# When the first six local units ask for their values: an attention, expert and mixer kernel on one core

## The chip, the core and the metric

The kernel runs on one core of a Trainium2 chip, as one program. What counts is its device time in microseconds, the median of several executions. The core has a matrix engine (PE, with its weight loads as PEld), VectorE (DVE), ScalarE (ACT), GpSimd (POOL), a queue that issues most transfers (SP), and 16 DMA engines that carry them from memory (HBM) to the on-chip buffer. Every engine works through its own list of instructions in order; semaphores tie the lists together.

## The reference

Three stages follow each other, for 4 sequences of 768 tokens:

```python
for c in range(nc):                                   # 24 chunks of 32 queries, 8 heads of 64
    k_full = concat([mem_k, k[l_start:r_end]])        # 8 memory slots, 16 tokens left, 8 right
    a = softmax(scale * q_c @ k_full.T)
    out[c] = a @ v_full
x = out.reshape(B, S, 512)
for e in range(4):                                    # experts: causal attention, top 2 of 4 per token
    a = softmax(causal(scale * (x @ wq[e]) @ (x @ wk[e]).T))
    y += gate[e] * (a @ (x @ wv[e]) @ wo[e])
u = y + mix(y, U, V)                                  # over the sequence, rank 32
return u + relu(u @ w_ch1) @ w_ch2
```

## The kernel before

The first stage is cut into *units*: one unit is one sequence, two heads and half of the sequence, so 8 per sequence and 32 in all. A unit has a query tile `q_t` (192 KB in the packed form of the first eight), a key tile `k_t` (220 KB) and a value tile `v_t` (288 KB). Its work is: two score groups (`local_scores`, tile `s` on PE, then `a` on VectorE and ACT, sums `rs` on VectorE, a scaling of `a` on GpSimd), two transposes (`local_turn`, tile `tp` on PE, copied to `at`), the values (`local_values`, tile `t` on PE from `at` and `v_t`), and a split of the result into two parts `xh` (ACT) and `xl` (VectorE) (`local_split`). These feed the projections of the second stage, `pqk` and `pv`.

The first six units, all of the first sequence, run in a loop of six rounds ahead of the main loop (`PRO = 6`). Round r calls `rnd` with unit r for loading and scores (`s_unit`), and unit r-1 for transposes and values (`o_unit`, `locs`). From round 2 on the unit's `xh` and `xl` go into the projection at once (`qk_begin`). Between the rounds the weights come in: four pieces of `wqk` of 256 KB (`load_weights` from table `WLOAD`), split into two parts by `split_weights`; two pieces `wvg`, cast on ACT and subtracted on GpSimd; the mixer's U and V (`fetch_mixer`, and `load_mixer`: a decode on ACT and VectorE, tiles `u_s` and `d_t`, then ACT's cast `vs` and twelve copies `v_st`, four on ACT and eight on GpSimd); and `tri_s`, from which VectorE makes `row_s`.

All of these go out on SP's list, except the first keys and the mask, which ACT issues. An issue takes one of eight semaphores in turn and waits until the transfer that had it before has landed, so eight transfers at most are under way. Value tiles of units 0 to 2 lie in a pool of three buffers; those of units 3 to 5 lie in buffers that the main loop uses later (`FIRST_V`). The lists of all engines are not written by hand: a scheduler puts the recorded operations in order when the program is built, so where an operation is recorded can move its neighbours.

Of the kernel before, what the change touches and what calls it, by code (L numbers as in the profile page):

```python
# [8 lines left out]
F32 = mybir.dt.float32  # L9
# [8 lines left out]
B, H, S, D = 4, 8, 768, 64  # L18
# [3 lines left out]
NG = S // GQ  # L22
GK = NMEM + LEFT + GQ + RIGHT
# [12 lines left out]
PRO = 6  # L36
NPACK = 8
NKEEP = 1
NIDLE = 4
WLOAD = {1: ((0,), ()), 2: ((1,), ()), 3: ((2, 3), ()), 5: ((), (0, 1))}  # L40
WSPLIT = {2: ((0,), ()), 3: ((1, 2), ()), 4: ((3,), ()), 5: ((), (0, 1))}
FILL = ((0, 0, 0, 2, 1, 2, 1, 1, 2, 3, 0, 2),
# [8 lines left out]
NVB = 3  # L51
# [64 lines left out]
def tile_chunk_attention__moe_attention__mixer(  # L116
# [20 lines left out]
    nc = tc.nc  # L137
# [287 lines left out]
    TL, TE, TQ = dict(tag="lt", bufs=2), dict(tag="ts", bufs=2), dict(tag="ts", bufs=2)  # L425
    with ExitStack() as p1:
        const = p1.enter_context(tc.tile_pool(name="const", bufs=1))
        loc = p1.enter_context(ExitStack())
        lin = loc.enter_context(tc.tile_pool(name="lin", bufs=NLIN, side="right"))
# [9 lines left out]
        ps = Banks(p1, "psq", "psc")  # L439
# [16 lines left out]
        def load_weights(qk, vg):  # L456
            for kt in qk:
                raws["qk", kt] = cw.tile([128, 512], F32, name="raw", tag="ac", bufs=NAC)
                nc.sync.dma_start(raws["qk", kt], wqk[kt])
            for i in vg:  # L460
                raws["vg", i] = cw.tile([128, 2, 260], F32, name="raw", tag="ac", bufs=NAC)
                nc.sync.dma_start(raws["vg", i], wvg[2 * i:2 * i + 2].rearrange("k p n -> p k n"))
# [37 lines left out]
        xh, xl, half = {}, {}, {}  # L500
        nhalf = [0]
# [4 lines left out]
        FIRST_V = {n: (cw, dict(tag="ac", bufs=NAC)) for n in (3, 4, 5)}  # L506

        def local_load(u):
            b, hp, hf = u
            gs = slice(hf * NG // 2, (hf + 1) * NG // 2)  # L510
            n = nhalf[0]
            qpool, qkw = FIRST_Q.get(n, (lin, dict(bufs=NKB)))
            kpool, kkw = FIRST_K.get(n, (lin, {}))
            vpool, vkw = FIRST_V.get(n, (lin, dict(bufs=NVB)))
            packed = n < NPACK
            q_t = qpool.tile([128, NG // 2, GQ] if packed else [128, NG // 2, 2, GQ], F32, name="q_t", **qkw)
            nhalf[0] += 1
            hold['q', n] = nc.sync.dma_start(q_t, qP[hp, hf] if packed else qT[b, hp][:, gs]).ins
            k_t = kpool.tile([128, KHALF], F32, name="k_t", **kkw)
            (nc.sync if n else nc.scalar).dma_start(k_t, kw[b, hp, hf])  # L520
            if nhalf[0] == 1:
                nc.scalar.dma_start(band_s[:, :2], band)
                for n, (lo, hi) in enumerate(((0, LEFT), (GK - NMEM - RIGHT, GK - NMEM))):
                    (nc.gpsimd.tensor_copy if n else nc.scalar.copy)(band_s[:, 2 + n], band_s[:, n])
                    nc.gpsimd.memset(band_s[:, 2 + n, lo:hi], NEG_LOCAL)
                nc.sync.dma_start(ident_s, ident)
            v_t = vpool.tile([GK, NG // 2, 2, D], F32, name="v_t", **vkw)
            nc.sync.dma_start(v_t, vw[b, hp][:, gs])
            half[u] = dict(packed=packed, q=q_t, k=k_t, v=v_t, a={}, at={}, ins=[])

        def keys(k_t, g):
            at = g // 2 * KPAIR + g % 2 * (GK - NB)
            return k_t[:, at:at + GK]

        def local_scores(u, qd):
            b, hp, hf = u
            w = half[u]
            s = ps.tile([128, 3, GK], F32, name="s", **TL)
            a = lwk.tile([128, 3, GK], F32, name="a")
            nm = sm.tile([128, 3], F32, name="nm")  # L540
            ss = sm.tile([128, 3], F32, name="ss")
            for j in range(3):
                k_g = keys(w["k"], qd * 3 + j)
                for own in (slice(0, 64), slice(64, 128)) if w["packed"] else (slice(0, 128),):
                    last = nc.tensor.matmul(s[own, j, :], w["q"][own, qd * 3 + j], k_g[own], start=True, stop=True).ins  # L545
            for j in range(3):
                g = hf * NG // 2 + qd * 3 + j
                bd = band_s[:, 2 if g == 0 else 3 if g == NG - 1 else g % 2]
                nc.vector.tensor_tensor_reduce(a[:, j, :], s[:, j, :], bd, op0=ALU.add, op1=ALU.min,  # L549
                                               scale=-scale, scalar=-NEG_LOCAL, accum_out=nm[:, j:j + 1])  # L550
            for j in range(3):
                nc.scalar.activation(a[:, j, :], a[:, j, :], AF.Exp, bias=nm[:, j:j + 1], scale=-1.0,  # L552
                                     accum_out=ss[:, j:j + 1])
            rs = sm.tile([128, 3], F32, name="rs")
            nc.vector.tensor_scalar(rs, ss, 1e-9, None, op0=ALU.add)
            nc.vector.reciprocal(rs, rs)  # L556
            nc.gpsimd.tensor_mul(a, a, rs[:, :, None].to_broadcast([128, 3, GK]))  # L557
            w["a"][qd] = a
            if nhalf[0] <= NKEEP and qd:
                keep_warm(last)  # L560

        def keep_warm(after):
            p = ps.tile([128, 512], F32, name="pwarm", **TQ)
            with tc.issue_after(after):
                for _ in range(NIDLE):
                    nc.tensor.matmul(p, warm[:, :128], warm, start=True, stop=True)

        def local_turn(u, qd):
            w = half[u]
            a = w["a"].pop(qd)  # L570
            tp = ps.tile([GK, 3, 128], F32, name="tp", **(TQ if nhalf[0] < PRO else TL))
            for j in range(3):
                nc.tensor.transpose(tp[:, j, :], a[:, j, :], ident_s)  # L573
            at = lwk.tile([GK, 3, 128], F32, name="at", bufs=NLT)
            w["ins"].append((nc.scalar.copy if qd < NLA else nc.vector.tensor_copy)(at, tp).ins)
            w["at"][qd] = at
# [305 lines left out]

        def rnd(new=None, old=None, s_unit=None, o_unit=None, fill1=(), fill2=(), down=None, then=None, late=(), locs=(), at=None):

            def urgent(kind):
                return tc.high_priority(URGENT[kind, *at]) if at and (kind, *at) in URGENT else ExitStack()

            if s_unit:  # L890
                local_load(s_unit)
                if then:
                    load_weights(*then)
                with urgent(0):
                    local_scores(s_unit, 0)
            turned = []
# [34 lines left out]
            def place(items):  # L931
                w = len(items) * 128
                for n, bank in enumerate(banks):
                    if used[n] + w <= 512:
                        used[n] += w
                        return n, bank[:, used[n] - w:used[n]]

            late = sorted(late, key=lambda v: (shared[v][0], shared[v][1]))
            while late:
                items = [v for v in late if v[:2] == late[0][:2] and shared[v][0] == shared[late[0]][0]]  # L940
                at = place(items)
                if at is None:
                    items = items[:1]
                    at = place(items)
                late = [v for v in late if v not in items]
# [73 lines left out]
        units = batch_half(0, 0) + batch_half(0, 1)  # L1019
# [4 lines left out]
        for r in range(PRO):  # L1024
            more = [lambda: qk_begin(0, 0, r - 2, pp)] if 2 <= r < KT + 2 else []
            if r == PRO - 1:
                more += [lambda t=t: v_proj(0, t) for t in range(3)]
            split = [lambda: split_weights(*WSPLIT[r])] if r in WSPLIT else []
            rnd(s_unit=units[r], o_unit=units[r - 1] if r else None, fill1=split, fill2=more, then=WLOAD.get(r), locs=units[r - 1:r] if r else ())
            if r == 3:  # L1030
                fetch_mixer()
            if r == 4:
                nc.vector.memset(rank_s, 0.0)
                nc.sync.dma_start(identb_s, identb)
                nc.sync.dma_start(tri_s, tri)
                nc.vector.memset(row_s[:, :S - 128], 0.0)
                nc.vector.tensor_copy(row_s[:, S - 128:], tri_s)
        load_mixer()
        old, turned, locs = None, [], []
        for b in range(B):  # L1040
# [7 lines left out]
            for r, (pr, i) in enumerate(ROUNDS[b]):  # L1048
                n = FILL[b][r]
                ending[0] = last and r >= 10  # L1050
                f1, f2, work = work[:n][:1], work[:n][1:], work[n:]
                ups, down = [], None
                for c, g, (turn, low, up) in sorted((c, g, MIX[c][g]) for c in range(max(0, b - 1), b + 1) for g in range(2)):
                    at = 12 * (b - c) + r
# [4 lines left out]
                    if at == low:  # L1059
                        assert down is None  # L1060
                        down = c, g
                f1 = ups + f1
                o_unit = s_at.get(r - 1) if r else before
# [4 lines left out]
                if r in SESSIONS[b]:  # L1068
                    rnd((b, pr, i), old, s_at.get(r), o_unit, f1, f2, down, late=now, locs=locs, at=(b, r))
                    turned, locs = wait, []  # L1070
# [3 lines left out]
                old = (b, pr, i)  # L1074
# [33 lines left out]
    with ExitStack() as p2:  # L1108
        hp = None
        wp2 = p2.enter_context(tc.tile_pool(name="wp2", bufs=1))  # L1110
        ps = Banks(p2, "psp", "psf")
# [42 lines left out]
        late = list(range(NEC, NCH))  # L1154
# [3 lines left out]
        for c in late:  # L1158
            nxt = c + 1 if c + 1 < NCH else None
            po = [ps.tile([128, CT], F32, name=f"po{m}", tag=f"po{m}", bufs=1) for m in range(KT)]  # L1160
            for f in range(FA):
# [6 lines left out]
                if nxt is None and f == FS:  # L1168
# [3 lines left out]
                    hp = p2.enter_context(tc.tile_pool(name="hp", bufs=1, side="right"))  # L1172
# [186 lines left out]
```

## Time and profile before

| what | value |
|---|---|
| median of 3 runs | 803.16 us (802.81 to 803.75) |
| the profiled execution | 804.32 us, of which 802.2 us from the first to the last instruction |
| busy: PE, DVE, ACT, POOL | 782.0, 619.5, 498.2, 160.9 us |
| chain of work that ended last | PE 81%, DVE 10%, DMA 4%, ACT 4% |
| granted clock of TensorE, mean | 0.995 |
| transfers on the main queue | 36416 packets, 76.21 MB |

Busy time is the time in which an engine works on at least one instruction. The chain is followed back from the last instruction: at each step to what released it, or to the instruction ahead of it on its engine. A difference between two executions shows first as a shift of like rows in the timelines.

### The profile page before, as it was taken

Reading aid. Unit: us, or ns where it says so; the run is one execution under the profiler, and the core shown is the slowest. Engines: PE = TensorE matmul, PEld = TensorE weight load, DVE = VectorE, ACT = ScalarE, POOL = GpSimd, SP = SyncE. Lnnn points to the kernel's source line nnn. Section 1 sums busy time; section 2 is a strip of 40 time slices with the busy share of each in tenths; the row PEclk is TensorE's granted clock in tenths of the full one; section 3 lists DMA queues with packets and bytes.
Section 4 is the critical chain, followed back from the end, with each engine's and each line's share of the span. In section 5 each row is a group of like instructions: output and inputs, shape, how many; then the busy total and the mean of one; then the engine's idle time right before and its main releaser. Section 6 shows DMA issues by size and latency. Waiting matters only on the chain.

```text
span 802.2 us, 17606 instructions
## 1 busy us (share of the span) xinstructions
PE 782.0 (97%) x6258; PEld 706.9 (88%) x6258; DVE 619.5 (77%) x2029; ACT 498.2 (62%) x1439; POOL 160.9 (20%) x244
## 2 busy tenths in 40 slices
PE   8999999999999998999999999999999999999997
PEld 5789998989989987888788888999999999999996
DVE  6697768887878679895569899989596695875956
ACT  6787767877777656755346668565464564555642
POOL 5554434544434433311000000000000000000000
PEclk9999999999999998999999999999999999999999
DMA  9443242433232132235056543103002030030211
GB/s 292 125 153 110 90 145 78 138 114 113 78 100 75 36 132 100 79 105 178 27 165 215 186 151 112 54 1 132 1 33 100 1 132 1 1 132 1 84 49 53
DMA packets 36791, 77.65 MB, mean 97 GB/s; under 512 B 4192, under 2 KB 12896, under 8 KB 35936
## 3 DMA queue, kind: packets, MB, share of 16 engines
q1 hardware_dynamic: 36416, 76.21, 29.4%
q8 instruction: 49, 0.80, 0.4%
q10 hardware_dynamic: 288, 0.32, 0.1%
q14 instruction: 38, 0.31, 0.1%
HBM read 60.79 MB, written 15.73 MB: 95 GB/s over the span
## 4 chain that ended last, share of the span: by engine, by line
PE 81%; DVE 10%; DMA 4%; ACT 4%; issue 1%; DVEq 0%; POOL 0%; ACTq 0%; SPq 0%
PE acc L1232 25%; PE ph L377 15%; PE t L881 7%; PE po L394 6%; PE pqk L604 6%; PE pv L644 5%; PE tpc L765 4%; PE s L545 3%; DMA raw<-in_w 2%; PE sc L684 2%; PE tp L573 2%; PE sc L686 2%; PE w1p L335 1%; DVE a L549 1%; ACT a L552 1%
## 5 line engine op out<-in xcount | busy, mean ns | idle before, releaser
L1232 PE MATMUL acc<-xhi,sw 128*128 128x256 f32 x1008 | 187.9, 282 | 0.1
L1232 PEld LDWEIGHTS acc<-xhi,sw 128*128 128x128 f32 x1008 | 159.3, 189 | 4.8 <-ACT xhi L1150 0.3
L1232 PE MATMUL acc<-xlo,sw 128*128 128x256 f32 x504 | 139.1, 282 | 0.2 <-DVE xlo L1151 0.2
L1147 DVE TENSOR_TENSOR sx<-t 128x256 f32<-128x256 f32 x180 | 67.5, 419 | 67.7 <-ACT t L1140 67.6
L1140 ACT ACTIVATE t<-ph 128x512 f32<-128x512 f32 x72 | 43.1, 598 | 100.3 <-PE ph L377 100.3
L1232 PEld LDWEIGHTS acc<-xlo,sw 128*128 128x128 f32 x504 | 95.5, 189 | 2.4 <-DVE xlo L1151 0.4
L1150 ACT CAST xhi<-sx 128x256 fp32r<-128x256 f32 x205 | 74.8, 407 | 22.1 <-DVE sx L1147 19.6
L742 POOL TENSOR_SCALAR ac<-ac,su,g 128x128 f32<-128x128 f32 (+5 forms) x92 | 68.1, 750 | 98.1 <-DVE su L740 33.6
L552 ACT ACTIVATE a<-a,nm 128x96 f32<-128x96 f32 x192 | 69.8, 366 | 16.9 <-DVE nm L549 16.4
L1151 DVE TENSOR_TENSOR xlo<-sx,xhi 128x256 fp32r<-128x256 f32 x205 | 76.5, 418 | 3.0 <-ACT xhi L1150 2.2
L377 PE MATMUL ph<-zh,wp_l 128*128 128x512 f32 x192 | 61.2, 398 | 0.0
L377 PE MATMUL ph<-zh,wp_h 128*128 128x512 f32 x192 | 60.9, 394 | 0.0
L707 ACT ACTIVATE ac<-ac,nmc 128x128 f32<-128x128 f32 (+5 forms) x72 | 47.9, 666 | 15.7 <-DVE nmc L705 15.2
L557 POOL TENSOR_TENSOR a<-a,rs 128x288 f32<-128x288 f32 x64 | 43.2, 679 | 68.2 <-DVE rs L556 21.0
L377 PE MATMUL ph<-zl,wp_h 128*128 128x512 f32 x176 | 55.5, 394 | 0.0
L765 PE MATMUL tpc<-ident_s,ac 128*128 128x128 f32 x336 | 52.3, 276 | 2.8 <-POOL kl L632 1.4
L545 PE MATMUL s<-k_t,q_t 128*128 128x96 f32 (+1 forms) x480 | 51.2, 267 | 2.7 <-DMA k_t<-in_kw 1.8
L545 PEld LDWEIGHTS s<-k_t,q_t 128*128 128x128 f32 (+1 forms) x480 | 46.2, 171 | 6.7 <-PE tp L573 2.2
L684 PE MATMUL sc<-kl,qs 128*128 128x384 f32 (+2 forms) x144 | 48.0, 338 | 2.1 <-DVE ath L767 1.0
L705 DVE CUSTOM_DVE_ANT_0 ac<-sc,row_s 128x128 f32<-128x128 f32 (+5 forms) x72 | 43.2, 617 | 5.0 <-PE sc L686 4.3
L765 PEld LDWEIGHTS tpc<-ident_s,ac 128*128 128x128 f32 x336 | 39.1, 142 | 8.9 <-issue 2.8
L549 DVE CUSTOM_DVE_ANT_0 a<-s,band_s 128x96 f32<-128x96 f32 x192 | 39.6, 250 | 7.1 <-PE s L545 6.3
(210 smaller groups left out, 1949.5 us busy)
## 6 DMA issues: line engine op xcount, KB each, us to landing
raw<-in_w SPq DMA_DIRECT2D x42, 256.0 KB, 3.7
v_t<-in_vw SPq DMA_DIRECT2D x32, 288.0 KB, 3.7
q_t<-in_qT SPq DMA_DIRECT2D x24, 384.0 KB, 3.2
k_t<-in_kw SPq DMA_DIRECT2D x31, 220.0 KB, 3.5
part<-o SPq DMA_DIRECT2D x24, 256.0 KB, 2.6
pt<-part SPq DMA_DIRECT2D x6, 1024.0 KB, 4.8
out<-pt SPq DMA_DIRECT2D x24, 256.0 KB, 2.3
raw<-in_w SPq DMA_DIRECT2D x11, 512.0 KB, 4.6
```

The costliest lines, as they stand in the source:

```text
L377: nc.tensor.matmul(p, w[f // 4][:, pr, fs], z[:, pr], start=(n == 0), stop=(n == 5))
L394: nc.tensor.matmul(po, w[f][:, ms], x, start=(start and n == 0), stop=(stop and n == 2))
L545: last = nc.tensor.matmul(s[own, j, :], w["q"][own, qd * 3 + j], k_g[own], start=True, stop=True).ins
L552: nc.scalar.activation(a[:, j, :], a[:, j, :], AF.Exp, bias=nm[:, j:j + 1], scale=-1.0, accum_out=ss[:, j:j + 1])
L684: nc.tensor.matmul(s[:, o:o + w], q, kl[b, e, hf][:, :w], start=True, stop=False)
L742: (nc.vector if ending[0] else nc.gpsimd).tensor_scalar(aa[h][:, :n], aa[h][:, :n], su[:, h:h + 1], gates[b, i // 3][:, i % 3, 2 * pr + h: ...
L765: hold['t', ROUNDS[b].index((pr, i))] = nc.tensor.transpose(tp[h][:, j * 128:(j + 1) * 128], aa[h][:, j * 128:(j + 1) * 128], ident_s).ins
L881: session.append(nc.tensor.matmul(*a, **kw).ins)
L1147: nc.vector.tensor_tensor(x, t[:, p[0], p[1]], t[:, q[0], q[1]], op=op)
L1150: nc.scalar.copy(hi, x)
L1151: nc.vector.tensor_sub(lo, x, f32(hi))
L1232: ended[0] = nc.tensor.matmul(acc[n][:, m], w[:, ms], x, start=(f == FA and u == 0 and m == 0), stop=(f == NF - 2 and u == 2 and m == 1)).ins
```

## The change

The table `WLOAD` becomes `LOADS`: for each of the six rounds a list of what is loaded, in that order, ahead of `rnd`: keys with queries (`'k'`), values (`'v'`) and weights (`'w'`), the first two with the number of the unit. `local_load` is split into `local_keys` and `local_v`, and keeps its name as a function that `rnd` still calls; it loads what the unit doesn't have yet. The unit's number is kept in its record, and two conditions that looked at the running count now look at that. Nothing else changes in the program's text.

```diff
--- before.py
+++ after.py
@@ -37,7 +37,7 @@
 NPACK = 8
 NKEEP = 1
 NIDLE = 4
-WLOAD = {1: ((0,), ()), 2: ((1,), ()), 3: ((2, 3), ()), 5: ((), (0, 1))}
+LOADS = {0: (('k', 0),), 1: (('k', 1), ('v', 0), ('w', ((0,), ()))), 2: (('k', 2), ('v', 1), ('w', ((1,), ()))), 3: (('k', 3), ('v', 2), ('w', ((2, 3), ()))), 4: (('k', 4), ('v', 3), ('v', 4)), 5: (('k', 5), ('v', 5), ('w', ((), (0, 1))))}
 WSPLIT = {2: ((0,), ()), 3: ((1, 2), ()), 4: ((3,), ()), 5: ((), (0, 1))}
 FILL = ((0, 0, 0, 2, 1, 2, 1, 1, 2, 3, 0, 2),
         (1, 2, 1, 1, 2, 0, 1, 1, 2, 0, 2, 1),
@@ -506,12 +506,17 @@
         FIRST_V = {n: (cw, dict(tag="ac", bufs=NAC)) for n in (3, 4, 5)}
 
         def local_load(u):
+            if u not in half:
+                local_keys(u)
+            if 'v' not in half[u]:
+                local_v(u)
+
+        def local_keys(u):
             b, hp, hf = u
             gs = slice(hf * NG // 2, (hf + 1) * NG // 2)
             n = nhalf[0]
             qpool, qkw = FIRST_Q.get(n, (lin, dict(bufs=NKB)))
             kpool, kkw = FIRST_K.get(n, (lin, {}))
-            vpool, vkw = FIRST_V.get(n, (lin, dict(bufs=NVB)))
             packed = n < NPACK
             q_t = qpool.tile([128, NG // 2, GQ] if packed else [128, NG // 2, 2, GQ], F32, name="q_t", **qkw)
             nhalf[0] += 1
@@ -524,9 +529,13 @@
                     (nc.gpsimd.tensor_copy if n else nc.scalar.copy)(band_s[:, 2 + n], band_s[:, n])
                     nc.gpsimd.memset(band_s[:, 2 + n, lo:hi], NEG_LOCAL)
                 nc.sync.dma_start(ident_s, ident)
-            v_t = vpool.tile([GK, NG // 2, 2, D], F32, name="v_t", **vkw)
-            nc.sync.dma_start(v_t, vw[b, hp][:, gs])
-            half[u] = dict(packed=packed, q=q_t, k=k_t, v=v_t, a={}, at={}, ins=[])
+            half[u] = dict(packed=packed, n=nhalf[0] - 1, q=q_t, k=k_t, a={}, at={}, ins=[])
+
+        def local_v(u):
+            b, hp, hf = u
+            vpool, vkw = FIRST_V.get(half[u]["n"], (lin, dict(bufs=NVB)))
+            v_t = half[u]["v"] = vpool.tile([GK, NG // 2, 2, D], F32, name="v_t", **vkw)
+            nc.sync.dma_start(v_t, vw[b, hp][:, hf * NG // 2:(hf + 1) * NG // 2])
 
         def keys(k_t, g):
             at = g // 2 * KPAIR + g % 2 * (GK - NB)
@@ -556,7 +565,7 @@
             nc.vector.reciprocal(rs, rs)
             nc.gpsimd.tensor_mul(a, a, rs[:, :, None].to_broadcast([128, 3, GK]))
             w["a"][qd] = a
-            if nhalf[0] <= NKEEP and qd:
+            if w["n"] < NKEEP and qd:
                 keep_warm(last)
 
         def keep_warm(after):
@@ -568,7 +577,7 @@
         def local_turn(u, qd):
             w = half[u]
             a = w["a"].pop(qd)
-            tp = ps.tile([GK, 3, 128], F32, name="tp", **(TQ if nhalf[0] < PRO else TL))
+            tp = ps.tile([GK, 3, 128], F32, name="tp", **(TQ if w["n"] < PRO - 2 else TL))
             for j in range(3):
                 nc.tensor.transpose(tp[:, j, :], a[:, j, :], ident_s)
             at = lwk.tile([GK, 3, 128], F32, name="at", bufs=NLT)
@@ -882,15 +891,13 @@
 
 
 
-        def rnd(new=None, old=None, s_unit=None, o_unit=None, fill1=(), fill2=(), down=None, then=None, late=(), locs=(), at=None):
+        def rnd(new=None, old=None, s_unit=None, o_unit=None, fill1=(), fill2=(), down=None, late=(), locs=(), at=None):
 
             def urgent(kind):
                 return tc.high_priority(URGENT[kind, *at]) if at and (kind, *at) in URGENT else ExitStack()
 
             if s_unit:
                 local_load(s_unit)
-                if then:
-                    load_weights(*then)
                 with urgent(0):
                     local_scores(s_unit, 0)
             turned = []
@@ -1026,7 +1033,12 @@
             if r == PRO - 1:
                 more += [lambda t=t: v_proj(0, t) for t in range(3)]
             split = [lambda: split_weights(*WSPLIT[r])] if r in WSPLIT else []
-            rnd(s_unit=units[r], o_unit=units[r - 1] if r else None, fill1=split, fill2=more, then=WLOAD.get(r), locs=units[r - 1:r] if r else ())
+            for kind, n in LOADS.get(r, ()):
+                if kind == 'w':
+                    load_weights(*n)
+                else:
+                    (local_keys if kind == 'k' else local_v)(units[n])
+            rnd(s_unit=units[r], o_unit=units[r - 1] if r else None, fill1=split, fill2=more, locs=units[r - 1:r] if r else ())
             if r == 3:
                 fetch_mixer()
             if r == 4:
```

The built programs differ in their lists only in the prologue; behind it every engine's list is the same. First SP, the issues ahead of the two `wvg` pieces, before (`raw64` are the mixer's U and V; `q_t_465` is unit 4, `q_t_559` unit 5):

```order
L479 DMA raw64_461<-in_mU 128x384
L479 DMA raw64_463<-in_mV 128x384
L518 DMA q_t_465<-in_qP 128x384
L520 DMA k_t_467<-in_kw 128x440
L528 DMA v_t_469<-in_vw 96x768
L1034 DMA identb_s_111<-in_identb 128x128
L1035 DMA tri_s_112<-in_tri 128x128
L518 DMA q_t_559<-in_qP 128x384
L520 DMA k_t_561<-in_kw 128x440
L528 DMA v_t_563<-in_vw 96x768
L462 DMA raw_565<-in_wvg 128x2x260
L462 DMA raw_567<-in_wvg 128x2x260
```

The same stretch after the change, up to the same two pieces:

```order
L523 DMA q_t_471<-in_qP 128x384
L525 DMA k_t_473<-in_kw 128x440
L538 DMA v_t_475<-in_vw 96x768
L538 DMA v_t_477<-in_vw 96x768
L538 DMA v_t_374<-in_vw 96x768
L1046 DMA identb_s_111<-in_identb 128x128
L1047 DMA tri_s_112<-in_tri 128x128
L523 DMA q_t_567<-in_qP 128x384
L525 DMA k_t_569<-in_kw 128x440
L538 DMA v_t_571<-in_vw 96x768
L462 DMA raw_573<-in_wvg 128x2x260
L462 DMA raw_575<-in_wvg 128x2x260
```

There are three value tiles in a row where there was one: `v_t_475` is unit 3's second copy, `v_t_477` unit 4's only one, `v_t_374` unit 2's second one. Nearer the start, after the change, from unit 0's second copy `v_t_202` on:

```order
L538 DMA v_t_202<-in_vw 96x768
L459 DMA raw_204<-in_wqk 128x512
L538 DMA v_t_206<-in_vw 96x768
L523 DMA q_t_277<-in_qP 128x384
L525 DMA k_t_279<-in_kw 128x440
L538 DMA v_t_281<-in_vw 96x768
L459 DMA raw_283<-in_wqk 128x512
L523 DMA q_t_370<-in_qP 128x384
L525 DMA k_t_372<-in_kw 128x440
L538 DMA v_t_285<-in_vw 96x768
L459 DMA raw_376<-in_wqk 128x512
L459 DMA raw_378<-in_wqk 128x512
```

`v_t_202` and `v_t_281` are second copies of units 0 and 1, `v_t_206` and `v_t_285` first copies of units 1 and 2; before, each of these units had one row. The number of a tile grows in the order in which the tiles are made.

Next ACT's list, from the split of unit 1 (`xh_362` before, `xh_366` after) to the copy ahead of unit 3's second transpose (`at_495` before, `at_503` after). Before:

```order
L592 CAST xh_362<-t_349 128x384
L486 CAST vs_765<-d_t_760 128x192
L575 COPY at_400<-tp_396 96x384
L496 CAST v_st_115<-vs_765 32x192 x3
L552 ACTIVATE a_472,ss_474<-a_472,nm_473 128x96 x3
L496 CAST v_st_115<-vs_765 32x192
L471 CAST wvg_h_119<-raw_565 128x520
L552 ACTIVATE a_498,ss_500<-a_498,nm_499 128x96 x3
L471 CAST wvg_h_119<-raw_567 128x520
L592 CAST xh_457<-t_444 128x384
L575 COPY at_495<-tp_491 96x384
```

After, beginning with the last two activations of unit 3 (`a_409`):

```order
L561 ACTIVATE a_409,ss_411<-a_409,nm_410 128x96 x2
L486 CAST vs_773<-d_t_768 128x192
L496 CAST v_st_115<-vs_773 32x192 x3
L601 CAST xh_366<-t_353 128x384
L496 CAST v_st_115<-vs_773 32x192
L584 COPY at_406<-tp_402 96x384
L561 ACTIVATE a_480,ss_482<-a_480,nm_481 128x96 x3
L561 ACTIVATE a_506,ss_508<-a_506,nm_507 128x96 x3
L471 CAST wvg_h_119<-raw_573 128x520
L471 CAST wvg_h_119<-raw_575 128x520
L601 CAST xh_463<-t_450 128x384
L584 COPY at_503<-tp_499 96x384
```

The cast `vs` and three `v_st` copies now stand ahead of unit 1's `xh`, and the copy `at_406`, that stood right behind `vs` as `at_400`, stands behind all four `v_st` and `xh`. The two `wvg` casts stand together behind both groups of activations.

## Rows read from the trace of the kernel before

**Rows 1.** Stretches: us, busy by engine (instructions), granted clock, DMA share, GB/s.
```profile
15.00:20.00 5.00, 4.60 (x62) 4.12 (x62) 4.60 (x21) 4.26 (x21) 4.75 (x5) 1.00 1.08 334
20.00:25.00 5.00, 3.77 (x42) 3.43 (x40) 4.17 (x24) 3.47 (x13) 3.47 (x7) 1.00 1.07 295
25.00:30.00 5.00, 4.52 (x62) 3.28 (x62) 2.94 (x13) 4.67 (x18) 4.71 (x8) 1.00 0.74 195
30.00:35.00 5.00, 5.00 (x61) 4.42 (x60) 2.59 (x13) 1.67 (x7) 1.81 (x3) 1.00 0.02 3
```

**Rows 2.** The page, transfers: line, engine, count, KB each, median us to landing.
```profile
v_t<-in_vw SPq DMA_DIRECT2D x32, 288.0 KB, 3.7
```

**Rows 3.** SP's issues in order of time: start us, us, line, tile.
```profile
12.29 0.33 SPq L520 DMA_DIRECT2D k_t<-in_kw  x1
14.79 0.33 SPq L1035 DMA_DIRECT2D tri_s<-in_tri  x1
17.13 1.95 SPq L462 DMA_DIRECT2D raw<-in_wvg  x2
```

**Rows 4.** Transfers, windows round those issues (18.7 last): KB, us to landing.
```profile
k_t<-in_kw SPq DMA_DIRECT2D x1, 220.0 KB, 5.7
tri_s<-in_tri SPq DMA_DIRECT2D x1, 32.0 KB, 6.1
raw<-in_wvg SPq DMA_DIRECT2D x1, 260.0 KB, 6.6
raw<-in_wvg SPq DMA_DIRECT2D x1, 260.0 KB, 7.0
```

**Rows 5.** Chain of waits: start us, us, what.
```profile
28.30 0.53 PE tp L573 x3
```

**Rows 6.** ACT in order of time: start us, us, instruction, [idle before it].
```profile
19.93 0.48 ACT L592 CAST xh<-t 128x384 fp32r<-128x384 f32 x1
21.84 0.35 ACT L486 CAST vs<-d_t 128x192 fp32r<-128x192 f32 x1 [1.43 <-DVE d_t L156]
22.09 0.47 ACT L575 COPY at<-tp 96x384 f32<-96x384 f32 x1
22.59 1.07 ACT L496 CAST v_st<-vs 32x192 fp32r<-32x192 f32 x3
26.89 0.61 ACT L471 CAST wvg_h<-raw 128x520 fp32r<-128x520 f32 x1
27.41 0.47 ACT L592 CAST xh<-t 128x384 fp32r<-128x384 f32 x1
27.78 0.47 ACT L575 COPY at<-tp 96x384 f32<-96x384 f32 x1
```

**Rows 7.** PE in order of time.
```profile
20.27 1.21 PE L545 MATMUL s<-k_t,q_t 64*64 64x96 f32 x24
22.71 0.50 PE L573 MATMUL tp<-ident_s,a 128*96 128x128 f32 x3 [1.23 <-ACT at L575]
25.90 0.92 PE L881 MATMUL t<-at,v_t 96*64 96x64 f32 x24
28.30 0.53 PE L573 MATMUL tp<-ident_s,a 128*96 128x128 f32 x3 [0.37 <-ACT at L575]
```

**Rows 8.** VectorE and GpSimd in order of time, near 19 us.
```profile
18.89 0.98 DVE L154 TENSOR_SCALAR u_s<-u_s 128x192 uint32<-128x192 uint32 x1
19.86 0.25 DVE L154 TENSOR_SCALAR d_t<-d_t 128x192 uint32<-128x192 uint32 x1
18.46 1.29 POOL L468 TENSOR_TENSOR wqk_l<-raw,wqk_h 128x512 fp32r<-128x512 f32 x1
```

**Rows 9.** PE in order of time, and the stretch behind it.
```profile
314.93 0.87 PE L831 MATMUL pyt<-ident_s,yT 128*128 128x128 f32 x6 [1.50 <-ACT ac L710]
317.38 0.58 PE L684 MATMUL sc<-kl,qs 128*128 128x256 f32 x1 [1.00 <-DVE ath L767]
...
318.00:325.00 7.00, 7.00 (x38) 6.74 (x38) 5.18 (x13) 4.01 (x11) 0.46 (x2) 0.60 0.14 56
```

## The prediction

> **What bounds the kernel now.** I read the table by stretches over the first 30 us first, for where the transfer engines are full [rows 1], then the transfers of that stretch with their landings [rows 2 to 4], the chain of waits [rows 5], and last the timelines of ACT and PE where the chain leaves one for the other [rows 6, 7].
>
> Over the whole span TensorE sets the time, but the edit is in the opening 30 us, and there the 16 DMA engines are full: from 15 to 25 us their share is above 1 at 334 and 295 GB/s; it falls to 0.74 only after 25 us [rows 1]. What arrives late is felt by SP's queue, which lets eight transfers be under way at a time. From 28.30 us the chain of waits runs on PE [rows 5]; ahead of that PE waits for ACT twice: 1.23 us ahead of a transpose at 22.71 and 0.37 us ahead of the one at 28.30 [rows 7]. That last row, `tp` at 28.30, is my gauge: behind it PE is busy without a gap (5.00 of the 5 us from 30 us on [rows 1]), and the engines hold the same rows in the same order to the end of the program. A delay of this row is a delay of the end.
>
> **What the change does.** The edit says that values are asked for one unit later. The listed order says more. `rnd` still calls `local_load`, which loads the values of a unit that has none; in round 1 to 4 the loop then calls `local_v` for the unit of the round before, which has them, and a second tile is made and filled. Only units 4 and 5 are loaded once. SP holds 36 value transfers where it held 32 (the 32: [rows 2]), so four of 288 KB are added, and nothing is taken away. PE reads the second copy of units 0 to 3.
>
> *The bytes.* 4 x 288 KB = 1152 KB, or 1.18 MB. At the best rate of this stretch, 334 GB/s [rows 1], that is 3.5 us of full engines, and there is no free place before about 27 us. What stands behind all four goes back 3.5 us: `tri_s`, unit 5's queries and keys, both `wvg` pieces. What stands behind two (the mixer's U and V, unit 4's queries and keys) goes back 1.8 us; behind one (the keys of units 2 and 3, three `wqk` pieces) 0.9 us. The Trainium skill, "DMA: Bandwidth & Descriptors", Specifications, gives 435 GB/s as the fabric's ceiling and about 358 GB/s as a core's share of HBM; an estimate by the first would make it 2.7 us and the forecast about 805.0, while the measured 334 lies by the second.
>
> *Which late ones are felt.* Unit 4's keys went out at 12.29 and took 5.7 us [rows 3, 4]: 18.0, now 19.8; PE asks for them at 20.27 [rows 7], so this is hidden by half a microsecond. `tri_s`: 14.79 + 6.1 = 20.9, now 24.4. Its reader on VectorE stands behind `xl` of unit 1, which I put at 24 to 24.5 below, so it hides too; without that cover it would hold VectorE up to 2 us. `wvg`: the first piece 17.13 + 6.6 = 23.7, now 27.3. The second went out at about 18.7 and took 7.0: 25.7. It was held back ahead of its issue, and now follows the first at once: 260 KB at 334 GB/s are 0.8 us, so 28.1; if it keeps its old distance, 29.2. Unit 2's used values stand ahead of `tri_s`, so land by 24.4, and PE takes them at 25.90 at the earliest [rows 7]. At the very start nothing moves: the first `wqk` piece keeps its place.
>
> *The order on ACT.* ACT's cast `vs` at 21.84 waits for VectorE's `d_t` (1.43 us idle), and `at` follows 0.25 us later [rows 6]; PE's transpose at 22.71 waits for exactly that `at`. In the new order three `v_st` copies, the cast `xh` of unit 1 and a fourth `v_st` come between. Their prices: 1.07 us for three `v_st`, a third of it, 0.36, for the fourth, and 0.37 for `xh` (27.41 to 27.78) [rows 6]. Sum 1.80 us. `xh` itself was done at 19.93, ahead of `vs`; now it stands behind `vs` and three copies, and `xl` and the projection wait for it; that is the same delay, not a second one.
>
> *When `vs` may start.* `d_t` ends VectorE's decode of the mixer's V. Unit 2's keys come 0.9 us later, and this pushes VectorE's rows; part is given back, since some sums `rs` stand farther from the ACT rows that they wait for. The trace shows no such mixture, so I bound it: 0 if all is given back, 0.9 if nothing is. I take 0.5, nearer the middle, because VectorE also stalls beside GpSimd: the shift at 18.89 took 0.98 us with GpSimd's 1.29 us subtraction under way from 18.46, where the like row took 0.25 [rows 8], and both lists now meet elsewhere. The Trainium skill, "SBUF — State Buffer", Who interferes with whom, has the two block each other fully; by that rule alone I would take the 0.9, and 805.4.
>
> *The sum.* `at` and PE's transpose: 1.8 + 0.5 = +2.3 us (1.8 to 2.7). PE then does the same rows up to the values of unit 2, 25.90 + 0.92 = 26.8 [rows 7], now 29.1. `xh` of unit 2 began at 27.41, 0.6 us after them, because ACT was still casting `wvg`: that 0.6 is given back, leaving +1.7 (1.2 to 2.1). By the other road, the last `wvg` cast starts at 28.1 (to 29.2) and `xh` 0.52 us behind it (26.89 to 27.41 [rows 6]): 28.6 (to 29.7), +1.2 to +2.3. The later of the two counts: between 1.3 and 2.4, and I take **+2.0 us**. The profiled execution took 804.32 us (span 802.2 and 2.1 around it), so 806.3; its median sister runs are 1.16 us lower at 803.16, so the forecast is 805.2 us. Later stages give nothing back: their loads wait for PE rows that all move along.
>
> **The rivals.**
> *The clock falls.* PE's idle stretch ahead of 22.71 was 1.23 us with the clock at 1.00 [rows 7, 1]; with +2.3 at one end and little at the other it is about 3 us. The one place in the trace where the granted clock falls in mid-program, to 0.60 in the mean of 7 us (so to 1.2 GHz for most of them), follows two idle stretches of 1.50 and 1.00 us [rows 9]. If it falls here, 0.4 x 7 = 2.8 us of clock are lost on work that then sets the pace, some 3 us more: 803.16 + 5 = 808.2. For it: the idle stretch is twice the longest of those. Against it: PE is busy on both sides, and a 1.23 did nothing. It decides if PE rows behind the wait take twice their time.
>
> *Hidden after all* (the other side: not slower). If VectorE loses nothing, `wvg` lands by 27.5 and ACT's casts fill idle time, the gauge slips under 1.6 us. For it: ACT holds the same rows in total, and GpSimd's `v_st` copies can begin earlier. Against: the four rows ahead of `at` alone cost 1.8 less 0.6. About +0.9: 804.0 us. It decides at `tp` before 29.9.
>
> *Faster.* Unit 0's values now stand ahead of two of unit 3's score products on PE, and VectorE's order is looser near 14 us, worth 0.2 to 0.3 us at most there; to gain 1.6 us the full DMA stretch would have to be no bound at all. About 801.5 us.
>
> **How the numbers follow.** About 0.2%, 1.6 us, is what a measurement of this kernel tells from no change. Forecast (1.3 to 2.4 us, 804.5 to 805.6) 0.50; clock 0.26; hidden 0.20; faster 0.04. A fifth of the forecast's case lies under 1.6 us, so slower is 0.40 + 0.26 = 0.66, the same 0.20 + 0.10 = 0.30, faster 0.04. The range leaves out faster and the lower quarter of hidden below, and the upper third of the clock's case above: 803.7 to 808.3.
>
> **What would show it.** Right: 36 value transfers and 1.18 MB more on the queue; DMA share near 1 until 28 to 29 us, not 25; ACT's wait at `vs` ending at 22 to 22.7; PE's wait ahead of its transpose near 3 us in place of 1.23; `wvg` casts back to back at 27 to 29 with idle time ahead of them; `tp` (28.30) at 30.0 to 30.6, and every later row behind by the same amount. Wrong: `tp` before 29.5; a granted clock under 1 in the 20 to 35 us stretch; or a later stage whose distance to before shrinks.

## The result and the profile after

The changed kernel took 808.47 us (median of 5 runs, 807.41 to 809.64) beside 803.75 us (802.81 to 805.89, 5 runs) of the kernel before: a ratio of 1.0054, with an interval of 1.0038 to 1.0070. Timed again beside the last experiments it took 806.94 us (805.03 to 809.09, 6 runs) beside 803.84 (802.38 to 805.54, 12 runs): 1.0044, 1.0027 to 1.0061. It is 3.1 to 4.7 us slower, where +2.0 was forecast. The profiled execution took 807.41 us (span 805.3, +3.1).

The page's row on the values, and the stretches, with the columns of [rows 1]:

```profile
v_t<-in_vw SPq DMA_DIRECT2D x36, 288.0 KB, 3.9
```

```profile
10.00:15.00 5.00, 2.93 (x38) 2.33 (x40) 4.02 (x27) 3.94 (x21) 3.62 (x5) 0.71 1.06 319
15.00:20.00 5.00, 5.00 (x53) 4.29 (x51) 3.67 (x15) 3.28 (x14) 3.38 (x5) 0.61 1.06 338
20.00:25.00 5.00, 3.94 (x60) 3.25 (x58) 3.06 (x17) 3.40 (x14) 3.19 (x6) 1.00 1.06 276
25.00:30.00 5.00, 4.05 (x52) 3.65 (x52) 3.05 (x19) 3.79 (x15) 3.81 (x10) 1.00 1.08 274
30.00:35.00 5.00, 4.37 (x37) 3.57 (x37) 2.79 (x18) 4.02 (x16) 3.08 (x4) 1.00 0.81 190
```

There are 36 transfers for 32 [rows 2]. The transfer engines are now full up to 30 us, where [rows 1] had 0.74 from 25 us on, but from 20 us on they move only 274 to 276 GB/s. The granted clock is 0.71 and 0.61 in two stretches where before it was 1.00: a fall to half (1.2 GHz) that the forecast put elsewhere.

The chain of waits of the changed kernel, up to the row that I use as a gauge (start us, us, what):

```profile
4.46 5.53 DMA v_t<-in_vw
...
10.45 5.41 DMA raw<-in_wqk
...
15.87 7.78 DMA v_t<-in_vw
...
23.67 6.36 DMA raw<-in_wvg
...
30.05 0.63 ACT wvg_h L471
30.68 0.37 ACT xh L601
31.05 0.38 ACT at L584
...
31.48 0.53 PE tp L582 x3
```

In the chain of before no transfer stands behind 8.73 us, and ACT's work led to the row at 28.30 [rows 5]:

```profile
26.98 0.52 ACT wvg_h L471
27.50 0.37 ACT xh L592
27.87 0.38 ACT at L575
```

Now one transfer hands over to the next, and the last is the second piece of `wvg`, which lands at 30.03. The gauge is 3.18 us late.

ACT and PE in order of time, as in [rows 6, 7]:

```profile
22.97 0.35 ACT L486 CAST vs<-d_t 128x192 fp32r<-128x192 f32 x1 [1.26 <-DVE d_t L156]
23.35 1.07 ACT L496 CAST v_st<-vs 32x192 fp32r<-32x192 f32 x3
24.45 0.48 ACT L601 CAST xh<-t 128x384 fp32r<-128x384 f32 x1
24.95 0.35 ACT L496 CAST v_st<-vs 32x192 fp32r<-32x192 f32 x1
25.33 0.48 ACT L584 COPY at<-tp 96x384 f32<-96x384 f32 x1
...
28.68 0.63 ACT L471 CAST wvg_h<-raw 128x520 fp32r<-128x520 f32 x1 [0.18 <-DMA raw<-in_wvg]
30.05 0.63 ACT L471 CAST wvg_h<-raw 128x520 fp32r<-128x520 f32 x1 [0.74 <-DMA raw<-in_wvg]
30.58 0.47 ACT L601 CAST xh<-t 128x384 fp32r<-128x384 f32 x1
```

```profile
11.38 1.53 PE L554 MATMUL s<-k_t,q_t 64*64 64x96 f32 x24 [2.21 <-DVE nm L558]
...
22.73 1.21 PE L554 MATMUL s<-k_t,q_t 64*64 64x96 f32 x24
25.95 0.51 PE L582 MATMUL tp<-ident_s,a 128*96 128x128 f32 x3 [2.00 <-ACT at L584]
...
31.48 0.53 PE L582 MATMUL tp<-ident_s,a 128*96 128x128 f32 x3 [0.63 <-ACT at L584]
```

The five instructions between `vs` and `at` are there as forecast. `xh` waits for the `wvg` cast ahead of it in ACT's queue, and that cast waits 0.74 us for its transfer.

### The profile page after: what moved, and what is told of

Its sections match the earlier page's. It is cut to its first block, busy times and chain, and to the rows that moved or that the text cites. A ratio compares the mean times of both kernels' runs of the same rounds, so it can differ in the third digit from the quotient of the medians.

```text
span 805.3 us, 17611 instructions
## 1 busy us (share of the span) xinstructions
PE 783.9 (97%) x6258; PEld 708.2 (88%) x6258; DVE 617.8 (77%) x2029; ACT 499.7 (62%) x1439; POOL 160.4 (20%) x244
## 4 chain that ended last, share of the span: by engine, by line
PE 80%; DVE 8%; DMA 6%; ACT 3%; issue 2%; SPq 0%; DVEq 0%; POOL 0%; ACTq 0%
PE acc L1244 25%; PE ph L377 15%; PE t L890 7%; PE po L394 6%; PE pqk L613 6%; PE pv L653 5%; PE tpc L774 4%; PE s L554 3%; DMA raw<-in_w 2%; PE sc L693 2%; PE tp L582 2%; PE sc L695 2%; DMA v_t<-in_vw 2%; PE w1p L335 1%; DMA raw<-in_wvg 1%
```

## The experiments

Theories. **Bytes**: the second copies delay what is queued behind them, above all the second `wvg` piece. **Order**: ACT's new order ahead of `at` costs the time. **Lateness**: values that land a round later do. **Clock**: the fall of the granted clock does. Ratios are against the kernel before (medians of 803.71 to 803.84 beside the experiments). The last column is read in the profiled executions: `tp` at the gauge, or `t` just behind it (31.71 before) where `tp` stands elsewhere in the order.

| run | median us (runs) | ratio (interval) | second `wvg` cast starts, us | PE rows at or behind the gauge, us |
|---|---|---|---|---|
| before | 803.75 (5) | | 26.89 | 28.30 |
| changed | 808.47 (5) | 1.0054 (1.0038 to 1.0070) | 30.05 | +3.18 |
| once | 804.10 (11) | 1.0015 (1.0001 to 1.0028) | 26.44 | +1.63 |
| xhfirst | 808.47 (6) | 1.0071 (1.0056 to 1.0085) | 30.15 | +3.28 |
| once_xh | 803.45 (12) | 1.0000 (0.9986 to 1.0015) | 25.61 | -0.19 |
| dead | 809.72 (6) | 1.0073 (1.0056 to 1.0089) | 32.17 | +6.94 |
| dead_small | 804.80 (11) | 1.0011 (0.9995 to 1.0027) | 28.03 | +1.14 |
| two | 806.23 (12) | 1.0039 (1.0022 to 1.0056) | 29.05 | +6.62 |
| wvg_early | 807.76 (6) | 1.0064 (1.0048 to 1.0080) | 23.80 | +4.79 |
| warm | 805.12 (11) | 1.0022 (1.0009 to 1.0035) | 30.59 | +2.63 |
| warm3 | 806.88 (7) | 1.0044 (1.0029 to 1.0059) | 30.25 | +3.38 |
| after_again | 806.94 (6) | 1.0044 (1.0027 to 1.0061) | 29.28 | +2.81 |

### Each value tile loaded once (once)

```diff
-            if 'v' not in half[u]:
+            if 'v' not in half[u] and u not in units[:PRO]:
```

> The change without its second copies: in the first six units each value tile is loaded once, one round later; ACT's list keeps the new order (vs and three v_st ahead of unit 1's xh). Theory of the bytes (the four added transfers carry the loss, by way of the late wvg pieces): wvg lands by 26.5 us, the gauge tp lies within 0.7 us of its 28.30 before, time within 0.8 us of the kernel before, clock at 1.00 from 10 to 20 us. Rival, the order on ACT: the loss is mostly that of the four rows ahead of the copy, so tp stays at 29.5 us or later and the time is 1.2 us or more above before.

Without the second copies 1.0015 is left of 1.0054. PE's gauge row, and GpSimd's rows ahead of it, by time:

```profile
29.93 0.54 PE L582 MATMUL tp<-ident_s,a 128*96 128x128 f32 x3 [0.40 <-POOL a L566]
```

```profile
26.72 2.53 POOL L472 TENSOR_TENSOR wvg_l<-raw,wvg_h 128x520 fp32r<-128x520 f32 x2
29.22 1.29 POOL L566 TENSOR_TENSOR a<-a,rs 128x288 f32<-128x288 f32 x2
```

The landing of `wvg` no longer decides (its second cast starts at 26.44). But 1.63 us stay, on the compute road: ACT's `at` is 1.57 us late (23.66 for 22.09 [rows 6]) behind three `v_st` and `xh`, and at the end the gauge waits for GpSimd, where both `wvg_l` subtractions now stand ahead of `a`. ACT's list is not quite that of the change either: `at` stands ahead of the fourth `v_st`, and both `wvg` casts stand between the two groups of activations. The two theories share this result: the row is where the rival put it, the median is only 0.4 us above before. Most of the loss needs the bytes.

### ScalarE's order put back, bytes left (xhfirst), and both undone (once_xh)

```diff
-            nc.scalar.copy(vs[:, 0], head)
+            with tc.issue_after(hold_x[1][0]):
+                nc.scalar.copy(vs[:, 0], head)
```

> The change with one more line: the cast vs is put behind unit 1's xh, so ACT's list is that of before at this place, and all 36 value transfers stay. Theory of the bytes: the second wvg piece still lands near 30 us and decides, tp stays at 31.2 to 31.6 us, time 3 to 5 us above before. Rival, the order on ACT: tp comes back to 29 to 30 us and the time to 1.7 us or less above before.

With `xh` ahead of `vs` PE's wait at the first transpose was gone, and nothing came of it. The chain of waits of this kernel ends as that of the change:

```profile
24.57 5.56 DMA raw<-in_wvg
...
30.15 0.63 ACT wvg_h L471
30.77 0.38 ACT xh L602
31.15 0.38 ACT at L585
...
31.58 0.53 PE tp L583 x3
```

> No duplicates, and ScalarE's first cast of the mixer held behind the second unit's xh, which puts xh and at back ahead of the casts. If ScalarE's order carries the 1.6 us that the kernel without duplicates still lost at 28.30 us: 28.3 to 28.8 and 803.0 to 803.9. If it is that queries and keys come ahead of the values in the first rounds: 29.5 to 30, and about 804.1 as there.

This is `once` with the same edit. PE's gauge row, by time:

```profile
28.11 0.53 PE L583 MATMUL tp<-ident_s,a 128*96 128x128 f32 x3 [0.80 <-ACT at L585]
```

The row stands where it stood before, and the ratio is 1.0000: the order that the change is named for, without the copies and with ACT's order kept, equals the kernel before. No version tried beats it. `xhfirst` and `once_xh` differ by the copies alone: 1.0071 and 1.0000. So the copies carry the loss, and values that are asked for a round later cost nothing that these runs can tell.

The 1.63 us of `once` at the gauge are gone with the one edit to ACT's order. That edit also moves GpSimd's list (one `a` stands ahead of the `wvg_l` again), so which of the two lists held the last part is not shown. By their times alone `once` and `once_xh` can't be told apart (the intervals overlap from 1.0001 to 1.0015); among executions with a mean granted clock of 1.000 the medians are 803.8 (`once`, 3), 802.9 (`once_xh`, 5) and 802.8 (before, 10). At the gauge, in one profile each, the order alone gives +1.6 and the bytes alone +3.3, and the two do not add up.

### Bytes without lateness (dead, dead_small) and half the copies (two)

In the kernel before, units 1 to 4 were to get this behind their keys (in `dead_small` one of the six groups, `:1`, is loaded instead of all):

```diff
+            if 1 <= n <= 4:
+                pb, php, phf = units[n - 1]
+                dpool, dkw = FIRST_V.get(n - 1, (lin, dict(bufs=NVB)))
+                spare = dpool.tile([GK, NG // 2, 2, D], F32, name="v_t", **dkw)
+                lo = phf * NG // 2
+                nc.sync.dma_start(spare[:, :NG // 2], vw[pb, php][:, lo:lo + NG // 2])
```

> The kernel before, with the four extra value transfers at the places of the change, into tiles that nobody reads: each unit still computes with the values that it loaded in its own round, so bytes are added and no value comes later. If the bytes carry the loss (they push the second pair of projection weights to about 30 us): the transposes that stood at 28.30 us come at 31.2 to 31.6, and the time is 806.5 to 808.5. If the loss comes of values that land a round later: 28.3 to 28.8, and 803.5 to 804.3.

The edit adds five transfers, not four. A loop in the first unit's branch uses the name `n` again and leaves it at 1, so unit 0 passes the condition too. The page's row:

```profile
v_t<-in_vw SPq DMA_DIRECT2D x37, 288.0 KB, 3.8
```

No product waits for a value here, and the loss is 6 us, more than that of the change and than the range of the bytes. But ACT's order is not that of before: the scheduler put all four `v_st` and `xh` ahead of `at` here too. So this run agrees with the bytes and does not part them from the order; `xhfirst` and `once_xh` do that. The gauge came late by a third road. PE's row, by time:

```profile
28.95 1.22 PE L551 MATMUL s<-k_t,q_t 64*64 64x96 f32 x12 [1.04 <-DMA k_t<-in_kw]
```

Unit 5's keys land at 28.8 us, where the changed kernel had them at 27.0, and the clock fell in the same stretch. They were as long under way (6.16 us for 6.1), but were issued 1.8 us later (22.65 for 20.87): with one more tile between them, their issue waited for unit 4's keys, eight transfers ahead, to land at 22.64.

> The same four extra transfers with a sixth of the bytes each (48 KB in place of 288 KB). If bytes cost: the transposes at 28.30 us come at most 0.6 us later, 803.4 to 804.4. If the number of transfers, or their places in the queue, costs: nearly as late as with whole tiles, 806 or more.

With 48 KB for 288 KB, and again five of them, 1.0011, an interval that holds 1. The row is 1.14 us late where at most 0.6 was expected, and the median of 804.80 lies above the range for bytes, far below the 806 of the other theory. Neither the number of transfers nor their slots explains 4 us.

```diff
-            if 'v' not in half[u]:
+            if 'v' not in half[u] and u not in units[2:PRO]:
```

> The changed kernel with only the values of units 0 and 1 loaded twice; units 2 to 5 load theirs once, a round later (34 transfers). If the weights' landing decides by the bytes ahead of it, it is half way (about 28.4 us) and the transposes come at about 30, no later than without any duplicate (29.93): 804.0 to 805.2. If each duplicate adds to the order's own delay: 30.7 or later, 805.3 to 806.5.

Two of the four copies cost 2.5 us of the 4.7 by the medians, and 1.0039 of 1.0054 by the ratios: more than the bytes theory had put on half of them. The median of 806.23 lies in the range of the other theory, that each duplicate adds to the order's own delay; this run does not decide between them. The profiled execution, with a span of 808.1 us, lies near the upper end of its runs (803.88 to 810.58). Its stretch, columns as in [rows 1]:

```profile
25.00:30.00 5.00, 2.84 (x10) 2.86 (x11) 2.99 (x15) 4.50 (x17) 4.47 (x11) 0.62 1.08 290
```

The clock fell to half at 26.2 us, within a wait of 3.03 us of PE, and the weights (cast at 29.05, with no wait for them) did not decide. In this execution the compute road at the lower clock did, so its +6.62 says nothing of half the bytes.

### Weights ahead of the values (wvg_early)

The `wvg` entry of `LOADS` moves from round 5 to round 4, ahead of the values.

> The change with the two wvg pieces asked for in round 4, ahead of the values of units 3 and 4 instead of in round 5; same bytes. Theory of the bytes by way of wvg: the pieces land near 22 us, tp is then set by the compute rows alone, which in the profile of the change were 0.6 us behind the wvg road: tp at 30.5 to 31.0 us, time 0.4 to 1 us below the changed kernel. Rival, the order on ACT alone sets it: no change of tp. Rival, wvg is the whole loss: tp at 29 or earlier.

The weights came early enough, and it helped nothing: the row is 4.79 us late, and the time does not differ from the changed kernel's by more than the noise. ACT and PE in order of time:

```profile
22.17 0.62 ACT L471 CAST wvg_h<-raw 128x520 fp32r<-128x520 f32 x1 [1.78 <-DMA raw<-in_wvg]
22.70 0.35 ACT L486 CAST vs<-d_t 128x192 fp32r<-128x192 f32 x1
23.80 0.62 ACT L471 CAST wvg_h<-raw 128x520 fp32r<-128x520 f32 x1 [0.76 <-DMA raw<-in_wvg]
24.45 1.07 ACT L496 CAST v_st<-vs 32x192 fp32r<-32x192 f32 x3
25.55 0.48 ACT L601 CAST xh<-t 128x384 fp32r<-128x384 f32 x1
```

```profile
26.54 0.85 PE L582 MATMUL tp<-ident_s,a 128*96 128x128 f32 x3 [4.15 <-ACT at L584]
```

The casts moved up in ACT's queue with their load, and now hold up `vs`, `xh` and `at`: PE waits 4.15 us, and its clock falls to half at 23.9 us.

### The clock (warm, warm3, after_again)

`warm` and `warm3` put idle products behind the first transposes of unit 0, seven and three; with seven the scheduler also moves `xh` ahead of the second `wvg` cast, with three no instruction of another engine changes its place. (One expectation below says unit 1; the edit takes unit 0.)

```diff
+            if w["n"] == 0 and qd == 0:
+                keep_warm(end, 3)
```

> The change with seven warm products on PE behind unit 0's first transposes, where PE is idle for 2.2 us waiting for unit 2's keys; they write a tile that nothing reads. Theory of the clock: the granted clock stays at 1.00 from 12 to 19 us, PE's rows from 14 to 22 us come 0.8 us or more earlier, and the time falls by 1 us or more against the changed kernel. Theory of the bytes: the clock may stay up, but tp waits for wvg at 30 us as before, so the time moves by less than 0.5 us.

The ratio went to 1.0022, against what the bytes theory expected, and the clock stayed at 1.00. But `xh` no longer stood behind the second cast, so this run mixes two causes. It does show the late weights without any fall of the clock: the row `t` is 2.63 us late, and ACT waits for the first piece:

```profile
29.48 0.62 ACT L471 CAST wvg_h<-raw 128x520 fp32r<-128x520 f32 x1 [1.08 <-DMA raw<-in_wvg]
```

The next two part the causes.

> The changed kernel with three idle products (about 0.7 us) in TensorE's 2.21 us idle behind unit 1's first transposes; no instruction of another engine changes its place, and no transfer. If the fall of the granted clock at 12 to 19 us costs nothing by itself (the weights' landing at 30 us decides): the transposes come at 31.2 to 31.6 even in an execution whose clock stays at 1.00 up to there, and the time is that of the changed kernel, 807.4 to 808.8. If the fall carries the loss: 30 or earlier and 804.5 to 806.

> The changed kernel as it is, beside the one above. Weights' landing: the transposes at 31.2 to 31.7 whether the clock fell ahead of them or not, 807.4 to 808.8. Clock: executions without a fall ahead of 20 us come at 806 or less.

`warm3`'s clock was 1.00 from 5 to 25 us, and it is as slow as the changed kernel beside it (806.88 and 806.94). ACT's row of the second weights and PE's gauge, by time:

```profile
30.25 0.63 ACT L471 CAST wvg_h<-raw 128x520 fp32r<-128x520 f32 x1 [0.70 <-DMA raw<-in_wvg]
```

```profile
31.68 0.53 PE L582 MATMUL tp<-ident_s,a 128*96 128x128 f32 x3 [0.33 <-ACT at L586]
```

In the second profiled execution of the changed kernel the clock did not fall at 12 us either, but at 24.2, within an idle stretch of 2.02 us, the place that the prediction named. The stretches and PE's rows:

```profile
20.00:25.00 5.00, 1.83 (x29) 1.49 (x27) 2.25 (x8) 2.95 (x9) 3.42 (x8) 0.92 1.07 262
25.00:30.00 5.00, 5.00 (x50) 4.57 (x48) 2.32 (x18) 3.52 (x14) 3.46 (x6) 0.74 1.09 296
```

```profile
21.35 1.21 PE L554 MATMUL s<-k_t,q_t 64*64 64x96 f32 x24 [1.16 <-DMA k_t<-in_kw]
24.57 0.85 PE L582 MATMUL tp<-ident_s,a 128*96 128x128 f32 x3 [2.02 <-ACT at L584]
...
31.11 0.53 PE L582 MATMUL tp<-ident_s,a 128*96 128x128 f32 x3 [0.24 <-ACT at L584]
```

Three executions with this order of rows, with the clock falling at 12.1, 24.2 and 26.1 us: the gauge is at 31.48, 31.11 and 31.68. The fall of the clock in the opening is real. In the first and the third it does not set the gauge; the weights' landing does (casts at 30.05 and 30.25). In the second the weights were cast at 29.28, and `xh` then waited 0.22 us for PE's products, so there the compute road, at the lower clock, came last, just behind the weights.

The times do not follow the bytes theory so plainly. Both medians lie under the 807.4 to 808.8 that it gave, and the two profiled executions, neither with a fall ahead of 20 us, took 805.03 and 805.95, at or below the 806 that the clock theory named. Their gauges are 2.81 and 3.38 us late all the same. What they lack is a later fall of the clock, near 320 us, that the profiled executions of the kernel before and of the first pair have.

## Why the prediction was right in direction and short in size

**The range.** The second median, 806.94, lies in 803.7 to 808.3; the first, 808.47, lies just above it, though its ratio on the 803.16 that the forecast was counted from makes 807.5. Either comes so near only by the part of the range that was put there for the clock rival; the forecast's own 804.5 to 805.6 held neither. That is luck in part. Of the signs of being right, the 36 transfers and the full engines came. ACT's wait at `vs` ended at 22.97 in the first profile and at 21.60 in the second, for 22 to 22.7; PE's wait was 2.0 us in both, not near 3; and `tp` came at 31.48 and 31.11, not at 30.0 to 30.6. Of the signs of being wrong two came: a granted clock under 1 from 20 us on (0.92 and 0.74 in `after_again`), and a distance that shrinks later.

**The gauge.** Right: PE's like rows behind it are 3.2 us late up to 298 us, where the changed kernel is spared 0.7 us of a wait of before; "later stages give nothing back" was not quite so. Near 320 us one thing moves the distance: before, the clock fell there [rows 9], and so it did in the changed kernel's first profile, where it is 2.5 us at 329 us and 3.1 at the end. In `after_again` it did not fall there, and the distance shrinks from 2.8 to 0.5 us. A single pair of profiles can thus be 2.3 us off by this alone; the ratios of many runs decide.

**Four second copies.** Right, and shown to be the cause: with ACT's order put back 1.0071 with them and 1.0000 without; five small ones in the kernel before give 1.0011.

**ACT's order, the first road.** Right in mechanism: +1.7 was forecast at the gauge, `once` showed +1.63, and `once_xh` took it away. That the sizes agree is partly luck, since in `once` the last wait was for GpSimd. Two parts were off. From `vs` to `at` the changed kernel took 2.36 us for 0.25, +2.1 for the 1.8 summed. And `d_t`, put at +0.5, was 1.13 us late in the first profile (22.97 for 21.84 [rows 6]), outside the bound of 0.9; there the clock had been low from 12.1 to 18.9 us. In `after_again`, without that fall, `vs` started at 21.60, and in `once` at 21.81: no delay at all. So PE's first transpose was 3.24 us late in the first profile (25.95 for 22.71) and 1.86 in `after_again`, for the 2.3 forecast. In the first profile this road alone would have put the gauge at about 30.9, +2.6, an estimate from the end of `t` (29.14 + 0.92) and the 0.89 us from `xh` to the gauge in before.

**`wvg`, the second road: the term that was mis-sized.** It was put at +1.2 to +2.3; it measured +3.2 in the first profile and came last there. Two steps of it failed. First, "at the best rate of this stretch, 334 GB/s [rows 1], that is 3.5 us": the first piece's cast started at 28.68 us with a wait for it, so it landed about 4.9 us later than the 23.7 of before, not 3.5. The rate of 20 to 30 us was 274 to 276 GB/s, and [rows 1] had already shown 295 for 20 to 25; I took the best row of a stretch where the next worse one was where the bytes would fall. 1.18 MB at 275 GB/s are 4.3 us; the other 0.6 is not explained. Second, the last piece "follows the first at once": the casts start 1.37 us apart, and the first of the two takes 0.6, so it landed at 30.03, neither at 28.1 nor at the 29.2 of the other bound. The Trainium skill, "DMA: Bandwidth & Descriptors", Specifications, has about 358 GB/s as a core's share of HBM; as a ceiling the traces agree (350 at most in the stretches of 5 us that were read), as a rate to count with it would have been further off than 334.

**What was said to be hidden.** `tri_s` was: its cast at 25.58 us follows `xl` without a wait. Unit 4's keys were in the first profile only because PE came late itself (22.73); they landed at 21.8, +3.8 us for the 1.8 forecast, and in `after_again` and `warm3` PE waited 1.16 and 0.75 us for them.

**The clock rival.** The mechanism came, in each of the three profiled executions, twice near the place that it was given (24.2 and 26.1 us) and once at 12.1. Its price of 3 us on top was not paid at the gauge: in two of them the weights came last, and in `after_again` the lower clock cost 0.2 us beyond them. 808.2 is near the first median by another road. In `two`, where the weights did not decide, the lower clock did.

**What stays open.** The two medians differ by more (+4.7 and +3.1) than the gauges of their profiles (+3.2 and +2.8). The executions of the changed kernel have mean granted clocks of 0.990 to 0.998, those of before 0.993 to 1.000; whether falls beyond the opening come more often in the one than in the other, and why some executions have the one near 320 us and some not, these runs do not tell. The kernel before shows what such falls go with: its executions at a mean clock of 1.000 have a median of 802.8 us (10 of them), those at 0.994 and below 805.7 (3). So a part of the 3.1 to 4.7 can be clock rather than the opening's delay; how much is open. `warm`, whose second copies stay, is at 804.8 in its five executions at 1.000, 2.0 above before.

## What to carry to other kernels

When a load is moved behind others, read from the order of instructions whether it is moved or made twice; here four tiles were loaded twice, and that was the whole loss once the order was put back. Count added bytes at the rate of the stretch into which they push the last of the queue, and see what waits behind the last byte on an in-order engine: a cast that waits for its weights holds every copy behind it.

## What the runs showed of the hardware

At a full share of the transfer engines the rate is not fixed: the stretches of 5 us between 5 and 30 us lie from 246 GB/s (`dead`) to 350 (`wvg_early`). The size of the packets may be a reason. Two windows of the changed kernel's transfers (packets, MB, rate, sizes), 10 to 20 and 20 to 30 us:

```profile
DMA packets 1791, 3.28 MB, mean 328 GB/s; under 512 B 212, under 2 KB 1031, under 8 KB 1790
...
DMA packets 1945, 2.75 MB, mean 275 GB/s; under 512 B 457, under 2 KB 1565, under 8 KB 1943
```

1.8 KB in the mean (3.28 MB in 1791 packets) go with 328 GB/s, 1.4 KB with 275. No run changes the packets alone, so the cause is not shown.

The same transfer takes longer or shorter with its company. Unit 4's keys, 220 KB, took 5.7 us with one value tile right behind them [rows 4], 5.6, 6.1 and 6.3 with two (`once_xh`, `once`, `two`), and 6.2, 7.5 and 7.9 with three (`xhfirst`, the changed kernel, `dead`). What is ahead of them differs in these runs too, so whether the tiles behind them slow them is not shown.

Idle time alone does not tell whether TensorE's clock falls. Its fall to half came 0.7 us behind an idle stretch of 2.21 us (the changed kernel, the row at 11.38), and within one of 2.02 us (`after_again`). It did not come with 2.00 us in the first of these executions (the row at 25.95, clock 1.00), nor with this one of `dead`, in a stretch (20 to 25 us) at 1.00:

```profile
22.77 0.71 PE L551 MATMUL s<-k_t,q_t 64*64 64x96 f32 x12 [2.67 <-DVE rs L562]
```

The same rows in another execution meet it in another place.
